# First batch of a band attention: transposing the weights unnormalized, and scaling x afterwards

## The chip, the core and the metric

The kernel runs on one core of one Trainium2 chip. The time is device microseconds of a whole execution; each kernel is timed in several runs and the median is given. The profile comes from one further execution, whose span (first to last instruction) is a little shorter than its time.

## The reference

Three stages follow one another, all in float32:

```python
# attention: 2 batches, 8 heads, 768 positions, head size 64
keep = is_global | is_local              # first 8 keys, and the last 96 keys before the query
scores = where(keep, q @ k.T / 8 + bias(head, distance), -1e9)
a = exp(scores - max(scores)); a = a / (sum(a) + 1e-9)
x = (a @ v) as 1536 tokens x 512
# feed-forward layer
h = x @ w_in                             # 512 -> 2048
x = (h * sigmoid(h)) @ w_out             # 2048 -> 512
# mixture of experts: 8 experts, each token to its best one
out[mask_e] = gate * (relu(x[mask_e] @ w1[e]) @ w2[e])
```

## The kernel before, in words

A tile is 128 queries; tiles 0 to 5 are the first batch, 6 to 11 the second. Because of the band a tile needs the keys of itself and of the tile before it (tile 0 only its own, so its score matrices are 128x128 and not 128x256). A unit is one pair of heads of one tile: unit u is head pair u%4 of tile u//4. The first batch has 24 units.

The order of the work is written out by hand. `slot_b(s)` issues the work of slot s, which belongs to several units at once: the score matmuls of unit s+1 (`emit_qk`), the bias and row maximum of unit s on VectorE (`emit_tb`, L178), the exponentials of unit s-1 on ScalarE (`emit_exp`, L188, which also sums each row into `ss`), the transposition of the weights of unit s-3 on TensorE (`emit_tr`, L212), the copy of the transposed weights out of PSUM (`emit_cp`, on ScalarE in slots 8 to 22, else on VectorE), and V's products of unit s-4 (`emit_px`, L227). V is the stationary operand there, so the result comes out transposed: features on the partitions, tokens along the free axis. In every slot from 8 to 22 VectorE also runs one operation of the decoding of the feed-forward weights (`dec_op`, L292 to L294), and in slots 0 to 6 TensorE runs two filler matmuls (`warm`, L82). Every instruction goes into the queue of its engine in this order, and each engine works its queue strictly in order.

Three pieces of this order belong to the normalization. `emit_mx` (L181) turns the row maximum into the bias of the exponential. `emit_dg` (L203 to L206) adds the small constant to the row sums of one unit, inverts them on VectorE, and lets GpSimd build for each head a diagonal matrix `dg` with these inverses. `emit_tr` then multiplies the weights with this diagonal matrix, which transposes and normalizes them in one float32 matmul. A float32 matmul appears in the trace as two instructions (so 8 for a unit with 4 blocks), a transposition through the identity, as in `gate1` (L392), as one.

When the last head pair of a tile is through (`hp==3`), `emit_xx` takes the product `pvt[n]` from PSUM through `put_xt`: ScalarE copies the high part into `xT` (L265), and VectorE subtracts it for the low part (L266). `emit_px` also calls `glob_v`, a GpSimd copy (L160) of V's rows for the global keys; `glob_k` (L157) does the same for the keys in each slot.

PSUM banks for scores, transposed weights and the like are handed out by `abank` in rotation, five of them during the slots; an instruction that takes a bank waits until the reader of its former content is done. Slots 0 to 23 run before the feed-forward layer; slots 24 to 27 are issued during its first two steps, beside its matmuls (L337 for the first layer, L357 to L359 for the second), which need `xT` and a PSUM bank named "s1" that tile 4's `pvt` also takes. During the 16 steps of the feed-forward layer's first chunk (tokens of tiles 0 to 3) VectorE decodes the rest of the weights. Later chunks and the experts follow.

Of the kernel before, what the change touches and what calls it, by code (L numbers as in the profile page):

```python
# [10 lines left out]
F32 = mybir.dt.float32  # L11
# [5 lines left out]
AF = mybir.ActivationFunctionType  # L17
ALU = mybir.AluOpType
AX = mybir.AxisListType
P = 128  # L20
# [3 lines left out]
def kernel(ctx, tc, qk, v, n_global, n_local, w_in, w_out, wg, w1, w2, out):  # L24
    nc=tc.nc
    B,NT=v.shape[0],v.shape[1]
    H=8; D=64; KC=4; FB=16; NTT=B*NT; LAG=2; LASTF=2; HB=6; PAIR=256; PX=4
# [3 lines left out]
    SB=24  # L31
    LT=3
# [10 lines left out]
    attn=es_a.enter_context(tc.tile_pool(name="attn",bufs=1,side="right"))  # L43
# [12 lines left out]
    ident=const.tile([P,P],F32,name="ident")  # L56
# [4 lines left out]
    def own_first(n): return n%3==1  # L61
# [10 lines left out]
    V=nc.vector; A=nc.scalar; G=nc.gpsimd; T=nc.tensor; S=nc.sync  # L72
# [6 lines left out]
    def warm(k):  # L79

        if not wm: wm.append(ps.tile([P,512],F32,tag="s1b",name="wm",bufs=1))
        for _ in range(k): T.matmul(wm[0].rearrange("p (a b) -> p a b",a=4),ones,ones[:,None,:].to_broadcast([P,4,P]),start=True,stop=True)  # L82
# [48 lines left out]
    def abank(shape,name):  # L131
        tg=atags[0][acnt[0]%len(atags[0])]; acnt[0]+=1
        return ps.tile(shape,F32,tag=tg,name=name,bufs=1)
# [24 lines left out]
    def glob_v(n):  # L158
        if n%NT in (0,NT-1): return
        if 4*n<SB: G.tensor_copy(vpr4[0:32,n%3,0:512],vpr4[0:32,(n-1)%3,0:512])  # L160
        else: V.tensor_copy(vpr[0:32,n%3],vpr[0:32,(n-1)%3])
    qp={}
    def emit_qk(n,hp,j):
        i=n%NT
        if (n,hp,j) in qp: return
        q=qp[n,hp,j]=abank([P,2,P],"qkp")
        sl=slice(0,2) if i else slice(0,1)
        w=ring[hp//2][j*D:(j+1)*D,hp%2]; z=ksl(n)
        T.matmul(q[:,sl],w[:,z,1],w[:,z:z+1,0] if i==0 else w[:,0:3:2,0] if z==0 else w[:,z-1:z+1,0],start=True,stop=True)  # L169
    def emit_tb(n,hp,j):  # L170
        i=n%NT; h=2*hp+j; q=qp.pop((n,hp,j))
        if j==0: tt[n,hp]=attn.tile([P,2,2,P],F32,tag="t",name="t",bufs=3) if 4*n>=SB else mp.tile([P,2,2,P],F32,tag="g",name="t",bufs=6)
        t=tt[n,hp]
        if h==0:
            mx[n]=attn.tile([P,H],F32,tag="mx",name="mx",bufs=2); ss[n]=attn.tile([P,H],F32,tag="ss",name="ss",bufs=2)
        sl=slice(0,2) if i else slice(0,1)
        tb=tabs[:,3:4,h,:] if i==0 else (tabs[:,1::-1,h,:] if i==1 else tabs[:,1:3,h,:]) if own_first(n) else tabs[:,0:2,h,:] if i==1 else tabs[:,2:0:-1,h,:]
        V.tensor_tensor_reduce(out=t[:,j,sl],in0=q[:,sl],in1=tb,scale=1.0,scalar=-3e38,op0=ALU.add,op1=ALU.max,accum_out=mx[n][:,h:h+1])  # L178
    def emit_mx(n,hp):
        h=2*hp+1  # L180
        V.tensor_scalar(out=mx[n][:,h-1:h+1],in0=mx[n][:,h-1:h+1],scalar1=-0.125,scalar2=float(np.log(1024.0)),op0=ALU.mult,op1=ALU.add)  # L181
    def emit_exp(n,hp):
        i=n%NT
        t=tt[n,hp]
        ce=1 if i==0 else 2
        for j in range(2):
            h=2*hp+j
            A.activation(out=t[:,j,:ce],in_=t[:,j,:ce],func=AF.Exp,scale=0.125,bias=mx[n][:,h:h+1],accum_out=ss[n][:,h:h+1])  # L188
    def emit_h(n,hp):
        t=tt[n,hp]; nch=ce=1 if n%NT==0 else 2  # L190
        x=attn.tile([P,2,2,nch,P],F16,tag="hl",name="hl",bufs=2); hl[n,hp]=x
        V.tensor_copy(x[:,:,0],t[:,:,:ce])
    def emit_l(n,hp):
# [2 lines left out]
        y=attn.tile([P,2,2,nch,P],F16,tag="pT",name="pT",bufs=3)  # L196
        pT[n,hp]=y
        S.dma_start_transpose(out=y.rearrange("p a b c d -> p (a b c) d"),in_=x.rearrange("p a b c d -> p (a b c d)"))
    dg={}
    def emit_dg(n,hp):  # L200

        s=ss[n][:,2*hp:2*hp+2]
        V.tensor_scalar(out=s,in0=s,scalar1=1024.0e-9,scalar2=None,op0=ALU.add)  # L203
        V.reciprocal(out=s,in_=s)
        d=attn.tile([P,2,P],F32,tag="t",name="dg",bufs=3); dg[n,hp]=d
        for j in range(2): G.tensor_scalar(out=d[:,j],in0=ident,scalar1=s[:,j:j+1],scalar2=None,op0=ALU.mult)  # L206
    def emit_tr(n,hp):

        t=tt.pop((n,hp)); d=dg.pop((n,hp)); ce=1 if n%NT==0 else 2
        m=abank([P,2,ce,P],"tp")  # L210
        for j in range(2):
            for c in range(ce): T.matmul(m[:,j,c],t[:,j,c],d[:,j],start=True,stop=True)  # L212
        y=attn.tile([P,2,ce,P],F32,tag="pT",name="pT4",bufs=3); pT[n,hp]=y
        return y,m
    def emit_cp(y,m,e):
        if e is V: V.tensor_copy(y,m)
        else: A.activation(out=y,in_=m,func=AF.Copy)
    def emit_px(n,hp):

        i=n%NT; ce=1 if i==0 else 2  # L220
        if hp==0: pvt[n]=ps.tile([P,KC,P],F32,tag="pv" if n%2 else "s1",name="px",bufs=1)
        y=pT.pop((n,hp))
        vb=[n%3] if ce==1 else [n%3,(n-1)%3] if own_first(n) else [(n-1)%3,n%3]
        for c in range(ce):
            for j in range(2):
                h=2*hp+j
                T.matmul(pvt[n][j*D:(j+1)*D,hp,:],vpr4[:,vb[c],h*D:(h+1)*D],y[:,j,c,:],start=(c==0),stop=(c==ce-1))  # L227
        if hp==3: glob_v(n)
    xlow=[]
    def emit_xx(n):  # L230
        put_xt(n,pvt[n],xlow if 4*(n+2)<SB else None)
    def emit_pv(n,hp):
        i=n%NT; ce=1 if i==0 else 2
        if hp==0: pvt[n]=ps.tile([P,H,D],F32,tag="pv",name="pv",bufs=1)
        y=pT.pop((n,hp))
        vb=[n%3] if ce==1 else [n%3,(n-1)%3] if own_first(n) else [(n-1)%3,n%3]
        for j in range(2):
            h=2*hp+j
            for c in range(ce):
                seq=[(0,0),(0,1),(0,2),(1,0),(1,1)]  # L240
                for k,(a,m) in enumerate(seq):
                    T.matmul(pvt[n][:,h,:],y[:,j,a,c,:],vpr[:,vb[c],m,h*D:(h+1)*D],start=(c==0 and k==0),stop=(c==ce-1 and k==4))  # L242
    rs={}
    def emit_rs(n,k):
        if k==0:
            rs[n]=attn.tile([P,H,1],F32,tag="rs",name="rs",bufs=2)
            V.tensor_scalar(out=rs[n][:,:,0],in0=ss[n],scalar1=1024.0e-9,scalar2=None,op0=ALU.add)
        else: V.reciprocal(out=rs[n],in_=rs[n])
    def emit_fin(n):
        r=rs.pop(n)  # L250
# [4 lines left out]
    def emit_xt(n):  # L255
# [2 lines left out]
        for k in range(KC):  # L258
            T.transpose(m[:,k,:],xa[:,2*k:2*k+2,:].rearrange("p a d -> p (a d)"),ident)
        put_xt(n,m)  # L260
    def put_xt(n,m,later=None):
        c,u=divmod(n,2)
        if u==0: xT[c]=mp.tile([P,2,KC,256],F32R,tag="xT",name="xT",bufs=3)
        sl=xT[c][:,:,:,u*P:(u+1)*P]
        A.activation(out=sl[:,0],in_=m,func=AF.Copy)  # L265
        def low(): V.tensor_tensor(out=sl[:,1],in0=m,in1=sl[:,0],op=ALU.subtract)  # L266
        if later is None: low()
        else: later.append(low)


    wraw={}; wol={}
# [357 lines left out]
    h1={}; hh={}; yp={}  # L629
# [248 lines left out]
    def want(s):  # L878
        while nl_[0]<=min(s,NS-1):
            load(nl_[0]); nl_[0]+=1  # L880
# [4 lines left out]
    npv=[SB]; fin=[]  # L885
    TB={s:[(0,2*s-2),(0,2*s-1)] for s in range(1,5)}
    for s,hs in ((5,range(3)),(6,range(3,6)),(7,range(6,8))): TB[s]=[(2,h) for h in hs]
    def slot_b(s):

        ev=[]  # L890
        n,hp=divmod(s,4); n1,h1=divmod(s-1,4); n3,h3=divmod(s-LT,4); n4,h4=divmod(s-LT-1,4)
        cur=s<SB; o1=0<=s-1<SB; o3=0<=s-LT<SB; o4=0<=s-LT-1<SB
        def a_():
            if s<SB-3: want(min(s+WL,SB-1))
            elif cur: want(s+3)
            if s==0:
                for j in range(2): emit_qk(n,hp,j)
            if cur: emit_tb(n,hp,0)
            if s+1<SB:
                for j in range(2): emit_qk(*divmod(s+1,4),j)  # L900
            if s<7: warm(2)
            if o3: cp[0]=emit_tr(n3,h3)
            if o1: emit_exp(n1,h1)
        ev.append(a_)
        def a2():
            if cur: emit_tb(n,hp,1); emit_mx(n,hp)
            if o3: emit_cp(*cp[0],A if DQ<=s<23 else V)
            if o1: emit_dg(n1,h1)
            if o4: emit_px(n4,h4)
            if xlow: xlow.pop()()  # L910
        ev.append(a2)
        def b_():
            if cur: glob_k(n,hp)
            if h4==3 and o4: emit_xx(n4)
            if s==0: table(slice(0,3))
            for d,h in TB.get(s,()): tab_heads(slice(0,2) if d==0 else slice(2,3),slice(0,2) if d==0 else slice(2,3),(h,))
            if hp==3 and 4*(n+1)<SB and cur: load_v(n+1)
        ev.append(b_)
        return ev
    cp=[None]  # L920
# [38 lines left out]
    with tc.manual_schedule():  # L959
# [11 lines left out]
        s=0  # L971
# [17 lines left out]
        for g in range(len(steps)+LAG):  # L989
            live=g<len(steps)  # L990
            if live:
                c,f=steps[g]
# [79 lines left out]
```

## Time and profile before

| | |
|---|---|
| time, median of 3 runs | 609.31 us (608.39 to 609.93) |
| profiled execution: its time, its span | 609.15 us, 607.4 us |
| busy over the span: TensorE (PE) | 590.5 us, 97% |
| weight loads of TensorE (PEld) | 498.5 us, 82% |
| VectorE (DVE) | 388.2 us, 64% |
| ScalarE (ACT) | 302.1 us, 50% |
| GpSimd (POOL) | 185.7 us, 31% |
| mean granted TensorE clock | 0.998 of full speed |

Times in the rows are microseconds from the span's start unless they are marked ns. A matmul's end is modelled, so the distance from one start to the next tells more than a duration. A mean in a group can hold instructions that waited inside the engine. Busy shares over the whole span are averages over stages that have different limits; the stage of the slots ends before 60 us.

### The profile page before, as it was taken

To read this page: it belongs to the slowest core of one execution; us is meant where nothing else is said; L and a number is where in the kernel's file an instruction comes from. 1 tells how busy PE (TensorE), PEld (TensorE's weight loads), DVE (VectorE), ACT (ScalarE), POOL (GpSimd) and SP (SyncE) were. 2 spreads that over 40 slices of the span, in tenths; PEclk is the share of its full clock that TensorE was granted. 3 is DMA by queue.
4 is the path that set the end of the run, shared out by engine and by line. 5 is a ranking of instruction groups with operands and counts; after the bars stand their busy time and mean duration, and the time that the engine had idled before them with its cause. 6 is when DMAs were issued, how large, how long until landed. Compare 5 with 4: busy or idle time off the path is not lost.

```text
span 607.4 us, 12066 instructions
## 1 busy us (share of the span) xinstructions
PE 590.5 (97%) x4078; PEld 498.5 (82%) x4078; DVE 388.2 (64%) x1074; ACT 302.1 (50%) x800; POOL 185.7 (31%) x232
## 2 busy tenths in 40 slices
PE   8998999999999999999999999999999999999995
PEld 4666888888888888888889999887888988888784
DVE  6888599998465655554543346646653877867940
ACT  7677334443444444343432325725653756776741
POOL 4678244444124341222120001212231432332321
PEclk9999999999999999999999999999999999999999
DMA  6554826788646666464434239309755558558500
GB/s 208 194 173 157 265 87 212 224 266 283 206 110 170 154 164 178 116 159 107 134 108 122 87 96 339 141 37 306 218 176 168 184 198 295 173 211 296 165 18 20
DMA packets 81226, 105.18 MB, mean 173 GB/s; under 512 B 29693, under 2 KB 44029, under 8 KB 81156
## 3 DMA queue, kind: packets, MB, share of 16 engines
q1 hardware_dynamic: 78292, 97.41, 52.0%
q0 software_dynamic: 2288, 6.39, 2.9%
q8 instruction: 34, 0.56, 0.4%
q10 hardware_dynamic: 576, 0.52, 0.3%
q14 instruction: 36, 0.29, 0.2%
HBM read 87.14 MB, written 17.99 MB: 173 GB/s over the span
## 4 chain that ended last, share of the span: by engine, by line
PE 68%; DVE 10%; issue 9%; ACT 5%; DMA 4%; POOL 3%; SPq 0%; POOLq 0%; DVEq 0%; ACTq 0%
PE s L337 17%; PE s L357 6%; PE s L358 5%; PE s L359 5%; PE h L640 4%; PE h L634 4%; PE qkp L169 4%; PE y L657 3%; PE y L659 3%; PE y L658 3%; PE tp L212 3%; POOL wol L321 2%; PE pv L242 2%; PE h L635 2%; DVE wt L294 2%
## 5 line engine op out<-in xcount | busy, mean ns | idle before, releaser
L337 PEld LDWEIGHTS s<-xT,wi 128*128 128x128 f32 x1152 | 147.3, 190 | 13.1 <-DVE g L346 6.0
L337 PE MATMUL s<-xT,wi 128*128 128x256 f32 x1152 | 152.2, 284 | 1.9 <-DVE xT L266 1.4
L342 DVE SCALAR_TENSOR_TENSOR s<-u,s 128x256 f32<-128x256 f32 x96 | 39.7, 426 | 81.4 <-ACT u L341 81.4
L341 ACT ACTIVATE u<-s 128x256 f32<-128x256 f32 x96 | 35.2, 381 | 113.6 <-PE s L337 112.7
L509 DVE TENSOR_TENSOR uq<-qr,uq 128x512 fp32r<-128x512 f32 x87 | 76.2, 898 | 7.1 <-ACT uq L508 4.3
L357 PE MATMUL s<-woh,g 128*128 128x512 f32 x192 | 79.2, 413 | 0.0
L358 PE MATMUL s<-woh,g 128*128 128x512 f32 x192 | 75.5, 393 | 0.0
L508 ACT ACTIVATE uq<-qr 128x512 fp32r<-128x512 f32 x112 | 66.4, 626 | 7.8 <-DMA qr<-in_w_dram 7.7
L346 DVE TENSOR_TENSOR g<-s,g 128x256 fp32r<-128x256 f32 x96 | 39.3, 422 | 31.6 <-ACT g L345 26.3
L657 PE MATMUL y<-uq,hh 128*128 128x512 f32 (+6 forms) x136 | 55.2, 406 | 0.0
L345 ACT ACTIVATE g<-s 128x256 fp32r<-128x256 f32 x96 | 35.6, 379 | 39.3 <-DVE s L342 39.3
L659 PE MATMUL y<-uq,hh 128*128 128x512 f32 (+6 forms) x136 | 53.7, 395 | 0.0
L658 PE MATMUL y<-uq,hh 128*128 128x512 f32 (+6 forms) x136 | 53.4, 393 | 0.0
L509 POOL TENSOR_TENSOR uq<-qr,uq 128x512 fp32r<-128x512 f32 x25 | 32.7, 1317 | 56.8 <-ACT uq L508 54.0
L188 ACT ACTIVATE t<-t,mx 128x256 f32<-128x256 f32 (+1 forms) x96 | 45.7, 480 | 0.4 <-DVE mx L181 0.4
L650 DVE SCALAR_TENSOR_TENSOR hh<-h,hh 128x224 fp32r<-128x224 f32 (+6 forms) x64 | 25.3, 395 | 31.8 <-ACT hh L649 31.8
L649 ACT ACTIVATE hh<-h 128x224 fp32r<-128x224 f32 (+6 forms) x64 | 23.2, 363 | 44.1 <-DVE h L647 23.8
L595 POOL DMA_INDIRECT out_dram<-y,ixt x17 | 17.6, 1036 | 80.3 <-ACT y L664 51.3
L357 PEld LDWEIGHTS s<-woh,g 128*128 128x128 f32 x192 | 36.3, 189 | 7.1 <-ACT u L341 2.0
L358 PEld LDWEIGHTS s<-woh,g 128*128 128x128 f32 x192 | 36.3, 189 | 5.0
L359 PE MATMUL s<-wolr,g 128*128 128x512 f32 x128 | 39.6, 391 | 0.0
L195 POOL TENSOR_TENSOR hl<-t,hl 128x512 f16<-128x512 f32 (+1 forms) x18 | 19.9, 1105 | 52.5 <-ACT gsm L435 16.4
(223 smaller groups left out, 1079.5 us busy)
## 6 DMA issues: line engine op xcount, KB each, us to landing
qr<-in_w_dram SPq DMA_DIRECT2D x128, 256.0 KB, 4.5
wolr<-wlo_d SPq DMA_DIRECT2D x64, 256.0 KB, 3.0
wiraw<-in_w_in_dram SPq DMA_DIRECT2D x16, 512.0 KB, 4.1
wraw<-in_w_out_dram SPq DMA_DIRECT2D x13, 512.0 KB, 4.5
ring<-in_qk_dram SPq DMA_DIRECT2D x22, 256.0 KB, 4.2
xe<-xe SPq DMA_DIRECT2D x7, 792.0 KB, 7.1
wlo_d<-wol SPq DMA_DIRECT2D x16, 256.0 KB, 2.9
xw<-xe SPq DMA_DIRECT2D x15, 264.0 KB, 4.7
```

The lines of the kernel that those rows point to most:

```text
L188: A.activation(out=t[:,j,:ce],in_=t[:,j,:ce],func=AF.Exp,scale=0.125,bias=mx[n][:,h:h+1],accum_out=ss[n][:,h:h+1])
L337: T.matmul(t,w[:,ww,kc,:],x[:,xx,kc,:],start=(k==0),stop=(k==11)); k+=1
L342: V.scalar_tensor_tensor(out=t,in0=u,scalar=1.0,in1=t,op0=ALU.add,op1=ALU.mult)
L346: V.tensor_tensor(out=g[:,1],in0=t,in1=g[:,0],op=ALU.subtract)
L357: T.matmul(o,g[u][:,0,sl],wh,start=(f==0),stop=False)
L358: T.matmul(o,g[u][:,1,sl],wh,start=False,stop=False)
L359: else: T.matmul(o,g[u][:,0,sl],wl,start=False,stop=(f==FB-1))
L508: A.activation(out=t[:,0],in_=r,func=AF.Copy)
L509: (G if (i%2 if pool is None else pool) else V).tensor_tensor(out=t[:,1],in0=r,in1=t[:,0],op=ALU.subtract)
L657: T.matmul(o,g[:,0,sl],w[:,0],start=(f==0),stop=False)
L658: T.matmul(o,g[:,1,sl],w[:,0],start=False,stop=False)
L659: T.matmul(o,g[:,0,sl],w[:,1],start=False,stop=(f==7))
```

## The change

For the first batch the row minimum of -0.125 times (score + bias) replaces the row maximum, so that it is the bias of the exponential as it stands; `emit_mx` is no longer called there. `emit_dg` and the diagonal matrices go. `emit_tr` transposes the raw exponentials through the identity. Once per tile, two slots after its last unit's scores, `emit_rs` inverts all eight row sums and GpSimd spreads them over 512 columns (64 per head); `emit_rb` transposes this spread tile in four pieces on TensorE and ScalarE copies it out; `emit_xx` multiplies the product `pvt` with it on VectorE, and `put_xt` is given GpSimd for both the high and the low part of `xT`. For tiles 0 to 3 `emit_rb` stands behind V's products of the tile's last unit and `emit_xx` one slot later; for tiles 4 and 5 (`own`) `emit_rb` comes one slot earlier and `emit_xx` directly behind the products, as before.

```diff
@@ emit_tb
+        if 4*n<SB: V.tensor_tensor_reduce(out=t[:,j,sl],in0=q[:,sl],in1=tb,scale=-0.125,scalar=3e38,op0=ALU.add,op1=ALU.min,accum_out=mx[n][:,h:h+1])
+        else: V.tensor_tensor_reduce(... as before ...)
@@ emit_exp
-            A.activation(..., func=AF.Exp,scale=0.125,bias=mx[n][:,h:h+1],accum_out=ss[n][:,h:h+1])
+            A.activation(..., func=AF.Exp,scale=-1.0 if 4*n<SB else 0.125,bias=mx[n][:,h:h+1],accum_out=ss[n][:,h:h+1])
-    def emit_dg(n,hp):
-        s=ss[n][:,2*hp:2*hp+2]
-        V.tensor_scalar(out=s,in0=s,scalar1=1024.0e-9,scalar2=None,op0=ALU.add)
-        V.reciprocal(out=s,in_=s)
-        d=attn.tile([P,2,P],F32,tag="t",name="dg",bufs=3); dg[n,hp]=d
-        for j in range(2): G.tensor_scalar(out=d[:,j],in0=ident,scalar1=s[:,j:j+1],scalar2=None,op0=ALU.mult)
@@ emit_tr
-            for c in range(ce): T.matmul(m[:,j,c],t[:,j,c],d[:,j],start=True,stop=True)
+            for c in range(ce): T.transpose(m[:,j,c],t[:,j,c],ident)
+    def emit_rb(n):
+        r=rs.pop(n)
+        m=abank([P,KC,P],"rb")
+        for k in range(KC): T.transpose(m[:,k,:],r[:,k*P:(k+1)*P],ident)
+        x=rb[n]=attn.tile([P,KC,P],F32,tag="t",name="xn",bufs=3)
+        A.activation(out=x,in_=m,func=AF.Copy)
     def emit_xx(n):
-        put_xt(n,pvt[n],xlow if 4*(n+2)<SB else None)
+        x=rb.pop(n)
+        V.tensor_tensor(out=x,in0=pvt[n],in1=x,op=ALU.mult)
+        put_xt(n,x,G)
@@ put_xt
+        if e: e.tensor_copy(sl[:,0],m)
+        else: A.activation(out=sl[:,0],in_=m,func=AF.Copy)
+        (e or V).tensor_tensor(out=sl[:,1],in0=m,in1=sl[:,0],op=ALU.subtract)
@@ slot_b, a2
-            if cur: emit_tb(n,hp,1); emit_mx(n,hp)
+            if cur: emit_tb(n,hp,1)
             if o3: emit_cp(*cp[0],A if DQ<=s<23 else V)
-            if o1: emit_dg(n1,h1)
+            if o3 and h3==3 and own(n3): emit_rb(n3)
             if o4: emit_px(n4,h4)
-            if xlow: xlow.pop()()
+            if o4 and h4==3 and not own(n4): emit_rb(n4)
+            if o5 and h5==3 and not own(n5): emit_xx(n5)
+            if o2 and h2==3:
+                for k in range(2): emit_rs(n2,k)
+                r=attn.tile([P,512],F32,tag="t",name="rx",bufs=3)
+                G.tensor_copy(r.rearrange("p (h d) -> p h d",h=H),rs[n2].to_broadcast([P,H,D])); rs[n2]=r
@@ slot_b, b_
-            if h4==3 and o4: emit_xx(n4)
+            if h4==3 and o4 and own(n4): emit_xx(n4)
```

## Rows read from the trace of the kernel before

**Rows 1.** Busy time of each engine by stretch, with granted clock and DMA
```profile
40.00:50.00 10.00, 9.70 (x84) 6.99 (x84) 9.26 (x36) 7.63 (x24) 7.47 (x15) 1.00 0.48 160
...
80.00:90.00 10.00, 9.93 (x59) 8.26 (x59) 9.31 (x18) 4.83 (x12) 4.10 (x4) 1.00 0.35 97
...
160.00:170.00 10.00, 10.00 (x64) 8.56 (x64) 2.92 (x12) 5.78 (x16) 0.00 (x0) 1.00 0.72 238
```

**Rows 2.** Chain that ended last, by time: start, length, engine, tile, line
```profile
11.10 0.45 PE tp L212 x4
...
21.29 1.13 PE tp L212 x8
...
36.12 1.09 PE tp L212 x8
37.20 0.59 PE px L227 x8
37.79 0.63 PE qkp L169 x4
38.42 1.10 PE tp L212 x8
...
58.03 0.61 PE px L227 x8
```

**Rows 3.** Timeline of TensorE behind the slots: start, length, line, tiles
```profile
164.73 0.66 PE L392 MATMUL gt<-ident,xr 128*128 128x128 f32 x4
165.14 0.48 PE L357 MATMUL s<-woh,g 128*128 128x512 f32 x1
```

**Rows 4.** Timeline of VectorE over slot 22
```profile
54.66 0.40 DVE L178 CUSTOM_DVE_ANT_1 t<-qkp,tabs 128x256 f32<-128x256 f32 x1
...
56.05 0.17 DVE L181 TENSOR_SCALAR mx<-mx 128x2 f32<-128x2 f32 x1
...
56.41 0.40 DVE L178 CUSTOM_DVE_ANT_1 t<-qkp,tabs 128x256 f32<-128x256 f32 x1
```

**Rows 5.** Timeline of ScalarE over parts of slots 12 and 22
```profile
30.05 0.60 ACT L265 ACTIVATE xT<-px 128x512 fp32r<-128x512 f32 x1
30.55 0.62 ACT L314 ACTIVATE wi<-wt 128x512 fp32r<-128x512 f32 x1
31.07 0.50 ACT L188 ACTIVATE t<-t,mx 128x256 f32<-128x256 f32 x1
...
54.08 0.60 ACT L217 ACTIVATE pT<-tp 128x512 f32<-128x512 f32 x1 [0.35 <-PE tp L212]
...
55.46 0.19 ACT L188 ACTIVATION_READ_ACCUMULATOR t<-t,mx 128x1 f32 x1
```

**Rows 6.** Instruction groups, 0 to 170 us: busy, mean ns, idle before
```profile
L206 POOL TENSOR_SCALAR dg<-ident,ss 128x128 f32<-128x128 f32 x48 | 28.4, 603 | 21.2 <-DVE ss L204 10.8 <-DVE mx L178 5.5 <-ACT g L345 2.3
...
L315 POOL TENSOR_TENSOR wi<-wt,wi 128x512 fp32r<-128x512 f32 x16 | 20.7, 1294 | 28.8 <-ACT wi L314 28.7
...
L160 POOL COPY vpr<-vpr 32x512 f32<-32x512 f32 x4 | 2.4, 600 | 0.0
```

**Rows 7.** Timelines of VectorE and TensorE, slot 23 to feed-forward step 1
```profile
59.29 0.69 DVE L266 TENSOR_TENSOR xT<-px,xT 128x512 fp32r<-128x512 f32 x1
...
64.98 0.74 DVE L346 TENSOR_TENSOR g<-s,g 128x256 fp32r<-128x256 f32 x2
...
72.40 0.69 DVE L266 TENSOR_TENSOR xT<-px,xT 128x512 fp32r<-128x512 f32 x1 [0.73 <-ACT xT L265]
73.01 0.69 DVE L292 TENSOR_SCALAR dct<-wiraw 128x512 int32<-128x512 int32 x1
...
60.04 3.13 PE L337 MATMUL s<-xT,wi 128*128 128x256 f32 x24 [1.42 <-DVE xT L266]
63.01 1.06 PE L212 MATMUL tp<-dg,t 128*128 128x128 f32 x8
...
66.26 3.13 PE L337 MATMUL s<-xT,wi 128*128 128x256 f32 x24
```

More of the change, by code (lines that the diff above doesn't have):

```diff
@@ L177, in emit_tb @@
         tb=tabs[:,3:4,h,:] if i==0 else (tabs[:,1::-1,h,:] if i==1 else tabs[:,1:3,h,:]) if own_first(n) else tabs[:,0:2,h,:] if i==1 else tabs[:,2:0:-1,h,:]
-        V.tensor_tensor_reduce(out=t[:,j,sl],in0=q[:,sl],in1=tb,scale=1.0,scalar=-3e38,op0=ALU.add,op1=ALU.max,accum_out=mx[n][:,h:h+1])
+        if 4*n<SB: V.tensor_tensor_reduce(out=t[:,j,sl],in0=q[:,sl],in1=tb,scale=-0.125,scalar=3e38,op0=ALU.add,op1=ALU.min,accum_out=mx[n][:,h:h+1])
+        else: V.tensor_tensor_reduce(out=t[:,j,sl],in0=q[:,sl],in1=tb,scale=1.0,scalar=-3e38,op0=ALU.add,op1=ALU.max,accum_out=mx[n][:,h:h+1])
     def emit_mx(n,hp):
@@ L187, in emit_exp @@
             h=2*hp+j
-            A.activation(out=t[:,j,:ce],in_=t[:,j,:ce],func=AF.Exp,scale=0.125,bias=mx[n][:,h:h+1],accum_out=ss[n][:,h:h+1])
+            A.activation(out=t[:,j,:ce],in_=t[:,j,:ce],func=AF.Exp,scale=-1.0 if 4*n<SB else 0.125,bias=mx[n][:,h:h+1],accum_out=ss[n][:,h:h+1])
     def emit_h(n,hp):
@@ L198, in emit_l @@
         S.dma_start_transpose(out=y.rearrange("p a b c d -> p (a b c) d"),in_=x.rearrange("p a b c d -> p (a b c d)"))
-    dg={}
-    def emit_dg(n,hp):
-        s=ss[n][:,2*hp:2*hp+2]
-        V.tensor_scalar(out=s,in0=s,scalar1=1024.0e-9,scalar2=None,op0=ALU.add)
-        V.reciprocal(out=s,in_=s)
-        d=attn.tile([P,2,P],F32,tag="t",name="dg",bufs=3); dg[n,hp]=d
-        for j in range(2): G.tensor_scalar(out=d[:,j],in0=ident,scalar1=s[:,j:j+1],scalar2=None,op0=ALU.mult)
     def emit_tr(n,hp):
-        t=tt.pop((n,hp)); d=dg.pop((n,hp)); ce=1 if n%NT==0 else 2
+        t=tt.pop((n,hp)); ce=1 if n%NT==0 else 2
         m=abank([P,2,ce,P],"tp")
         for j in range(2):
-            for c in range(ce): T.matmul(m[:,j,c],t[:,j,c],d[:,j],start=True,stop=True)
+            for c in range(ce): T.transpose(m[:,j,c],t[:,j,c],ident)
         y=attn.tile([P,2,ce,P],F32,tag="pT",name="pT4",bufs=3); pT[n,hp]=y
@@ L228, in emit_px @@
         if hp==3: glob_v(n)
-    xlow=[]
+    rb={}
+    def emit_rb(n):
[4 more added lines that the diff above has]
+        A.activation(out=x,in_=m,func=AF.Copy)
     def emit_xx(n):
-        put_xt(n,pvt[n],xlow if 4*(n+2)<SB else None)
+        x=rb.pop(n)
+        V.tensor_tensor(out=x,in0=pvt[n],in1=x,op=ALU.mult)
+        put_xt(n,x,G)
     def emit_pv(n,hp):
@@ L246, in emit_rs @@
             rs[n]=attn.tile([P,H,1],F32,tag="rs",name="rs",bufs=2)
-            V.tensor_scalar(out=rs[n][:,:,0],in0=ss[n],scalar1=1024.0e-9,scalar2=None,op0=ALU.add)
+            V.tensor_scalar(out=rs[n][:,:,0],in0=ss[n],scalar1=1e-9 if 4*n<SB else 1024.0e-9,scalar2=None,op0=ALU.add)
         else: V.reciprocal(out=rs[n],in_=rs[n])
@@ L260, in emit_xt, with put_xt @@
         put_xt(n,m)
-    def put_xt(n,m,later=None):
+    def put_xt(n,m,e=None):
         c,u=divmod(n,2)
@@ L264, in put_xt @@
         sl=xT[c][:,:,:,u*P:(u+1)*P]
[L265 to L268, printed above, removed]
+        if e: e.tensor_copy(sl[:,0],m)
+        else: A.activation(out=sl[:,0],in_=m,func=AF.Copy)
+        (e or V).tensor_tensor(out=sl[:,1],in0=m,in1=sl[:,0],op=ALU.subtract)
     wraw={}; wol={}
@@ L887, with own @@
     for s,hs in ((5,range(3)),(6,range(3,6)),(7,range(6,8))): TB[s]=[(2,h) for h in hs]
+    def own(n): return 4*(n+2)>=SB
     def slot_b(s):
         ev=[]
+        n5,h5=divmod(s-LT-2,4); o5=0<=s-LT-2<SB
         n,hp=divmod(s,4); n1,h1=divmod(s-1,4); n3,h3=divmod(s-LT,4); n4,h4=divmod(s-LT-1,4)
-        cur=s<SB; o1=0<=s-1<SB; o3=0<=s-LT<SB; o4=0<=s-LT-1<SB
+        n2,h2=divmod(s-2,4); cur=s<SB; o1=0<=s-1<SB; o2=0<=s-2<SB; o3=0<=s-LT<SB; o4=0<=s-LT-1<SB
         def a_():
```

## The prediction

> **What bounds the kernel now.** I read the busy times by stretch first, then the chain that ended last, then the timelines of each engine over one slot. In the stretches the reader is to see three stages: during the slots (the row of 40 to 50 us) TensorE and VectorE are both nearly full, ScalarE and GpSimd three quarters; at 80 to 90 us, in the feed-forward layer's first chunk, TensorE and VectorE are both full, the latter with decoding; at 160 to 170 us TensorE alone is [rows 1]. Two full engines don't tell which one sets the pace; the chain does. In the middle of the slots it never leaves TensorE: transposition, V's products, scores, next transposition, with no gap, 38.42 - 36.12 = 2.30 us from slot to slot, of which 1.09 are the transposition, 0.59 V's products and 0.63 the scores [rows 2]. From the transposition of slot 8 (21.29) to the end of V's products of slot 23 (58.03 + 0.61 = 58.64) the 16 slots take 37.35 us, 2.33 each, so stalls are small there; slots 3 to 7 take 21.29 - 11.10 = 10.19 us [rows 2]. So the change works on the stage where the bound is, and on its longest term. What follows, the decoding and the later chunks, it leaves as it is; it can only start earlier.
>
> **Transposition (TensorE).** A full unit has 8 instructions through the diagonal, 1.09 us from the first to the next operation [rows 2]. Through the identity it has 4. The trace has such a group of four: 164.73 to 165.14, 0.41 us to the next start, and that next matmul is 0.48 long, stretched by the change of kind [rows 3]. I take 0.45, so 0.64 less per full unit; the 4 units of tile 0 have half the blocks and 0.45 now [rows 2], some 0.22 less each. New is one group of four per tile for the spread sums, 0.45, or 0.11 per slot. TensorE's slot becomes 0.63 + 0.45 + 0.59 + 0.11 = 1.78 us.
>
> **VectorE.** A slot from one first `emit_tb` to the next took 1.75 us (54.66 to 56.41), of which 0.36 (56.05 to 56.41) are the bias, the constant and the inversion, all of which go; 1.39 stay [rows 4]. The low part of xT also goes, 0.69 per tile [rows 7]. New per tile are the product with the spread sums, which I set at the same 0.69 (same 512 columns, one operand in PSUM too), and one pair of constant and inversion, at most the 0.36. That is 1.39 + 1.05/4 = 1.65 a slot against 1.75 + 0.69/4 = 1.92. Row minimum with another scale instead of row maximum is the same instruction, so I cost it at nothing; if it were slower, it has 0.2 of room before VectorE sets the pace.
>
> **ScalarE.** Copy and both exponentials take 54.08 to 55.65, 1.57 us. The copy of the spread sums replaces that of the high part, 0.50 per tile, 0.13 a slot; five weight splits of 0.52 fall in the 16 slots, 0.16 a slot [rows 5]. Sum 1.86, the same before and after. That was 0.47 under TensorE; now it is the highest of the engines, and this is what is late next.
>
> **GpSimd.** 48 diagonal matrices of 603 ns go, 28.4 us. New per tile are the spread copy, the high part's copy and the low part's subtraction. The subtraction is like L315, 1.29; the copies lie between the 0.60 of L160 (512 columns, a plain copy) and four times the 603 ns of a diagonal's 128 columns, 2.4 [rows 6]. I take 0.6 to 0.7, as the row nearest to it is a copy. Then 2.6 us a tile, 0.65 a slot, replace 1.2 a slot. For tiles 0 to 3 the sums are inverted two slots before they are transposed, some 4 us, which hides even a copy of 2.4. For tile 4 there is one slot, with tile 3's two xT operations and a weight split ahead in GpSimd's queue; there TensorE, with the transposes and V's products of slots 22 and 23 behind the wait, can lose 0 to 1.3 us, and I take 0.2 within the coupling below.
>
> **The new wait.** ScalarE's copy of the spread sums stands behind V's products and four transposes: 0.59 + 0.45 - 0.49 (the copy in front of it, from the rows above) = 0.55 us if ScalarE is right behind TensorE, with the next exponentials queued behind it and the products of later units behind those. It comes once in 4 slots, 0.14 a slot; if ScalarE is late by that much anyway, it costs nothing. The shift by one bank in `abank` lets the transposes of the next slot wait for the second `emit_tb` and not for the first; VectorE, now the least loaded of the three, should be ahead of it, and I take nothing, at most one decode and one `emit_tb`, about 1 us a tile or 0.25 a slot.
>
> **Sum.** Slots 8 to 23: 1.86 + 0.14 = 2.00 a slot against 2.33, 16 x 0.33 = 5.3 us. Bounds: 1.86, no coupling, 7.5; 2.2 with both waits in full, 2.1. Slots 3 to 7: 4 x 0.22 from tile 0's units, 0.64 for the first full one, up to 0.36 of VectorE's chain where slot 7 waits for it, less 0.45 for the first spread sums: 1.4, between 0.8 and 1.7. Junction to the feed-forward layer: its first matmul waited 1.42 us for ScalarE's copy and then VectorE's subtraction from tile 4's bank [rows 7]; one VectorE operation remains, 0.7 less. Step 0 has two transpositions in front of the matmuls of step 1 (63.01 to 66.26); they lose 1.28, but the first bank is only free when L346's first half is done, 64.98 + 0.37 = 65.35, so 0.9 [rows 7]. In step 1 the decoding begins at 73.01, behind tile 5's subtraction at 72.40, which had waited 0.73 for ScalarE [rows 7]; the product can take that place, 0.6. Together 2.2, bounds 1.2 and 2.3. Total 8.9 us, from 4.1 to 11.5. Made on the profiled execution: 609.15 - 8.9 = 600.3; the median is 0.16 higher, so 600.4, with 605.2 and 597.8 as the ends. VectorE's decoding from 73 us on fills it (9.31 of 10) [rows 1] whenever it starts, so I expect the gain to reach the end whole.
>
> **Rivals.**
> First: the waits bind. The slots hang on a chain across the engines (bank shift, spread copy, GpSimd at tile 4) at 2.2 a slot, and the small terms come at their lower ends: 605.2. For it speaks that three engines are within 0.21 of each other; against it, that transposition, copy and product are whole slots apart, which leaves each engine a lead.
> Second: the coupling is nothing and ScalarE runs through at 1.86: 597.8. The wait of 0.35 that it has before a copy in slot 22 [rows 5] shows it already following TensorE, so it would have to fall behind first.
> [...]
> [...]
> Fourth: the gain is given back, because weights for the decoding arrive no earlier. Then about 609. Against it: DMA is at 0.48 of its time during the slots [rows 1], and VectorE starts decoding at 73.01 straight behind its own subtraction, not behind a transfer [rows 7].
>
> **How the numbers follow.** Forecast 0.60, first rival 0.18, second 0.10, clock 0.08, given back 0.04. The time is the forecast's, 600.4. The range takes in the first and second rival, 597.5 to 605.6, and leaves out 0.12. Within 0.3% (1.8 us, about what this kernel's measurement can tell from no change) lies only the fourth: faster 0.88, same 0.04, slower 0.08.
>
> **What would show it.** In the profile after: L212 with 88 instructions instead of 176, four in 0.4 to 0.45 us; slots of 2.0 us in the middle, with ScalarE in the chain where TensorE alone was; V's products of slot 23 ended by 52; the first feed-forward matmul about 0.7 behind them; decoding begun at about 64 and the same length from there. Wrong would be: a granted clock under 1.00 between 15 and 55 us, slots over 2.2 with TensorE waiting for `mx` or for GpSimd, or a decoding that waits for DMA.

## The result, and the profile after

The changed kernel takes 598.5 us (median of 4 runs, 597.71 to 599.75) beside 608.99 us for the kernel before on the same chip; the ratio is 0.9828, interval 0.9806 to 0.985. The forecast was 600.4, the range 597.5 to 605.6. The profiled execution of after took 599.75 us with a span of 598.0, that of before 609.15. TensorE is busy for 98% of the span, VectorE for 63%, ScalarE for 50%, GpSimd for 29%.

The busy times by stretch of the kernel after answer to [rows 1]; the columns are the same. A second slot stretch, 30 to 40 us, is added.

```profile
30.00:40.00 10.00, 10.00 (x89) 6.46 (x88) 8.68 (x31) 9.68 (x30) 7.83 (x16) 1.00 0.73 239
40.00:50.00 10.00, 9.53 (x85) 6.10 (x84) 7.89 (x30) 8.92 (x29) 5.85 (x9) 1.00 0.51 170
...
80.00:90.00 10.00, 9.95 (x66) 8.90 (x66) 9.26 (x17) 3.71 (x10) 5.04 (x4) 1.00 0.68 221
```

TensorE has no idle time between 30 and 40 us; VectorE fell from 9.26 to 7.89 between 40 and 50, ScalarE rose from 7.63 to 8.92, being asked for the same work in fewer microseconds. The granted clock stays at 1.00. At 80 to 90 us the stage behind is as it was.

TensorE's timeline of the kernel after, from the first transposition to the feed-forward layer: start, length, line, tiles, and in brackets the idle time ahead of it and what ended that. It answers to [rows 2] and to TensorE's part of [rows 7].

```profile
11.40 0.38 PE L205 MATMUL tp<-ident,t 128*128 128x128 f32 x2
...
20.44 0.63 PE L205 MATMUL tp<-ident,t 128*128 128x128 f32 x4 [0.34 <-DVE mx L178]
...
28.22 0.66 PE L205 MATMUL tp<-ident,t 128*128 128x128 f32 x4
28.81 0.66 PE L220 MATMUL px<-pT,vpr 128*64 128x128 f32 x8
29.40 0.70 PE L169 MATMUL qkp<-ring 64*128 64x256 f32 x4
30.03 0.66 PE L205 MATMUL tp<-ident,t 128*128 128x128 f32 x4
...
47.46 0.66 PE L205 MATMUL tp<-ident,t 128*128 128x128 f32 x4
48.59 0.66 PE L227 MATMUL rb<-ident,rx 128*128 128x128 f32 x4 [0.47 <-DVE mx L178]
...
50.35 0.66 PE L220 MATMUL px<-pT,vpr 128*64 128x128 f32 x8
51.87 3.14 PE L338 MATMUL s<-xT,wi 128*128 128x256 f32 x24 [0.86 <-DVE xn L232]
...
57.19 3.13 PE L338 MATMUL s<-xT,wi 128*128 128x256 f32 x24
```

A slot is 30.03 - 28.22 = 1.81 us where it was 2.30. Read by starts, since a modelled end lies behind the next start (28.22 + 0.66 = 28.88 against 28.81): the transposition takes 28.81 - 28.22 = 0.59, V's products 0.59, the scores 0.63. No bracket stands on any of them, so TensorE has no idle time between them.

VectorE's timeline of the kernel after at the end of step 1 answers to the row at 73.01 in [rows 7]: decoding begins at 63.47, straight behind the product that took the subtraction's place.

```profile
62.87 0.68 DVE L232 TENSOR_TENSOR xn<-px,xn 128x512 f32<-128x512 f32 x1
63.47 0.69 DVE L293 TENSOR_SCALAR dct<-wiraw 128x512 int32<-128x512 int32 x1
```

The same points of both traces, subtracted, give where the time came from (before, after, won, forecast; us). The transposition of slot 3 begins at 10.94 in TensorE's timeline of before; the chain of [rows 2] enters it at 11.10.

| Section | before | after | won | forecast |
|---|---|---|---|---|
| entry to the transposition of slot 3 | 10.94 | 11.40 | -0.46 | 0 |
| slots 3 to 7 | 21.29 - 10.94 = 10.35 | 20.44 - 11.40 = 9.04 | 1.31 | 1.4 |
| slots 8 to 23, to the wait ahead of the first feed-forward matmul | 60.04 - 1.42 - 21.29 = 37.33 | 51.87 - 0.86 - 20.44 = 30.57 | 6.76 | 5.3 |
| that wait | 1.42 | 0.86 | 0.56 | 0.7 |
| step 0 | 66.26 - 60.04 = 6.22 | 57.19 - 51.87 = 5.32 | 0.90 | 0.9 |
| step 1 to the first decode | 73.01 - 66.26 = 6.75 | 63.47 - 57.19 = 6.28 | 0.47 | 0.6 |
| rest of the profiled execution | 609.15 - 73.01 = 536.14 | 599.75 - 63.47 = 536.28 | -0.14 | 0 |
| sum | 609.15 | 599.75 | 9.40 | 8.9 |

The profiled execution of after is the slowest of its four, so this pair shows 9.40 us where the medians lie 10.5 apart.

### The profile page after: what moved, and what is told of

It reads as the page before. It is cut to its first block, busy times and chain, and to the rows that moved or that the text cites. A ratio compares the mean times of both kernels' runs of the same rounds, so it can differ in the third digit from the quotient of the medians.

```text
span 598.0 us, 11816 instructions
## 1 busy us (share of the span) xinstructions
PE 583.9 (98%) x4014; PEld 490.0 (82%) x4014; DVE 378.9 (63%) x1014; ACT 300.8 (50%) x800; POOL 172.1 (29%) x202
## 5 line engine op out<-in xcount | busy, mean ns | idle before, releaser
L510 DVE TENSOR_TENSOR uq<-qr,uq 128x512 fp32r<-128x512 f32 x87 | 71.1, 840 | 7.5 <-ACT uq L509 4.7
```

What stands on the lines that cost most here:

```text
L510: (G if (i%2 if pool is None else pool) else V).tensor_tensor(out=t[:,1],in0=r,in1=t[:,0],op=ALU.subtract)
```

## The experiments

The theory: the slots are faster because TensorE's slot is shorter. The rival that grew out of the runs: much of it is the small work taken from VectorE, which the forecast had put off the path. All edits are to the kernel after unless it says otherwise; medians are given with the ratio to the kernel before in the same job, which took 608.86 to 609.27.

**The old work put back on scratch tiles** (bias, constant and inversion on VectorE, two diagonals on GpSimd per unit; nothing reads them):

```diff
+ def emit_dg(n,hp):   # s and d: tiles of their own
+     V.tensor_scalar(out=s,in0=ss[n][:,2*hp:2*hp+2],scalar1=1024.0e-9,scalar2=None,op0=ALU.add)
+     V.reciprocal(out=s,in_=s)
+     for j in range(2): G.tensor_scalar(out=d[:,j],in0=ident,scalar1=s[:,j:j+1],scalar2=None,op0=ALU.mult)
  if cur:
      emit_tb(n,hp,1)
+     V.tensor_scalar(out=y,in0=mx[n][:,2*hp:2*hp+2],scalar1=-0.125,scalar2=float(np.log(1024.0)),op0=ALU.mult,op1=ALU.add)
...
+ if o1: emit_dg(n1,h1)
```

> The changed kernel with the removed side work put back on scratch tiles: per unit the bias operation, the constant and the inversion on VectorE and the two diagonal matrices on GpSimd, none of them read by anything. The transposes stay single. Theory (the slots run at TensorE's pace, so what VectorE and GpSimd were spared is not the gain): VectorE's slot grows from about 1.65 to 2.0 us against TensorE's 1.81 plus a quarter of 0.59, so 598.5 to 600.5 us. Rival (the relief of VectorE and GpSimd is the gain): 605 us or more, most of the way back to 609.

Measured: 612.15, ratio 1.0049 (1.0032 to 1.0066), slower than the kernel before, which neither theory had. Its timeline, all engines:

```profile
30.79 0.60 POOL L160 COPY vpr<-vpr 32x512 f32<-32x512 f32 x1
...
30.80 2.01 DVE L918 TENSOR_SCALAR my<-mx 128x2 f32<-128x2 f32 x1
...
31.34 0.20 POOL L157 COPY ring<-ring 128x32 f32<-128x32 f32 x1
31.52 1.26 POOL L322 TENSOR_TENSOR wi<-wt,wi 128x512 fp32r<-128x512 f32 x1
...
34.06 0.66 PE L205 MATMUL tp<-ident,t 128*128 128x128 f32 x4 [1.32 <-DVE mx L178]
```

An operation on 2 columns, 0.17 us elsewhere, takes 2.01: it ends at 32.81, when GpSimd's three operations in a row end (31.52 + 1.26 = 32.78). The next `emit_tb` is queued behind it, and TensorE's transposes wait 1.32 for that. But GpSimd carried the old and the new work at once here (9.67 of 10 us at 40 to 50), which neither kernel does, so the run shows that such a wait occurs and not its share; the next ones separate the parts.

**The transposition as a two-pass matmul** again, all else kept:

```diff
- T.transpose(m[:,j,c],t[:,j,c],ident)
+ T.matmul(m[:,j,c],t[:,j,c],ident,start=True,stop=True)
```

> The changed kernel with each transposition as an ordinary float32 matmul with the identity, so two instructions again; nothing goes back on VectorE or GpSimd. Theory (TensorE's pace): 1.09 for 0.59 us per full unit, half of that for tile 0, 20 x 0.50 + 4 x 0.25 = 11 us more, 608.5 to 610. Rival (relief of the other engines): 599 to 602.

Measured: 608.36, ratio 0.9997 (0.9984 to 1.0009). TensorE's timeline:

```profile
33.33 1.16 PE L205 MATMUL tp<-ident,t 128*128 128x128 f32 x8
...
35.64 1.16 PE L205 MATMUL tp<-ident,t 128*128 128x128 f32 x8
```

The slot is 2.31 again. Without the single-pass transposes nothing is won.

**Each transposition issued twice**:

```diff
- for c in range(ce): T.transpose(...)
+ for c in [c for c in range(ce) for _ in range(2)]: T.transpose(...)
```

> The changed kernel with each transposition of the weights issued twice into the same place. Measures what one transposition costs where the slots run at TensorE's pace. 88 instructions more. If one costs 0.146 us (four in 0.585, as in the slots after): +12.8 us, 611.3. If 0.104 (four in 0.41 us, as the prediction read it behind the slots): +9.2, 607.7. If ScalarE had become the bound with TensorE 0.08 below it, as the prediction said, 1.3 us less than either.

Measured: 607.41, ratio 0.9973 (0.9961 to 0.9984), 8.9 us above the kernel after, 8.9 / 88 = 0.101 for each added transposition. TensorE's timeline, then the busy times of that stretch:

```profile
32.87 1.09 PE L205 MATMUL tp<-ident,t 128*128 128x128 f32 x8
...
35.11 1.09 PE L205 MATMUL tp<-ident,t 128*128 128x128 f32 x8
```

```profile
30.00:40.00 10.00, 10.00 (x89) 7.01 (x88) 6.62 (x23) 8.11 (x24) 6.25 (x11) 1.00 0.55 185
```

Slots of 2.24 against 1.81: four more transposes cost 0.44 at once, and they cost it although all other engines had room. So TensorE is the bound of the slot after the change. And 0.11 each, four of them 0.44, leaves 0.59 - 0.44 = 0.15 that a group pays once. About 1.03 of 2.24 us are transposes here and the clock stays at 1.00.

**The transposes of the spread sums issued twice** (`for k in (0,0,1,1,2,2,3,3)`):

> The changed kernel with the four transposes of the spread sums issued twice. Theory (TensorE's pace, no slack): 24 instructions more at 0.146 us, of which those of tile 5 stand beside the feed-forward matmuls: +2.9 to 3.5 us, 601.4 to 602. Rival of the prediction (ScalarE is the bound at 1.86 to 2.00 a slot and TensorE has room): under +1 us.

Measured: 602.63, ratio 0.9893 (0.9877 to 0.991). TensorE's timeline:

```profile
25.18 0.66 PE L205 MATMUL tp<-ident,t 128*128 128x128 f32 x4
...
26.36 1.09 PE L227 MATMUL rb<-ident,rx 128*128 128x128 f32 x8
...
28.02 0.66 PE L205 MATMUL tp<-ident,t 128*128 128x128 f32 x4
```

That slot is 2.84 against 28.22 - 25.83 = 2.39 after, 0.45 more. Four such slots are 1.8 us, and the group of tile 5, in step 1, is 0.4. Decoding begins at 65.00, 1.53 later than after, although the transposition of slot 3 came 0.63 earlier (10.77), so 2.16 are lost between these two points: the rival's "under +1 us" is out. The medians lie 4.1 apart; what adds the rest stays open.

**Only the transposes, on the kernel before** (diagonals still built; the exponentials' bias holds a constant per head pair):

```diff
- T.matmul(m[:,j,c],t[:,j,c],d[:,j],start=True,stop=True)
+ T.transpose(m[:,j,c],t[:,j,c],ident)
```

> The kernel before with one edit: the weights of the first batch go through the identity and not through the diagonal matrix, which is still built and read by nothing. Left out of the computation: the normalization of the first batch; each head pair is divided by a constant near its mean row sum (in the exponential's bias) so that the experts get about the same numbers of tokens. Side work on VectorE and GpSimd is that of before. Theory (TensorE was the bound, and the others follow close behind): slots at the highest of TensorE 1.81, VectorE 1.92, GpSimd 1.95 a slot, so 600 to 602 us. Rival (small operations of VectorE and the diagonals of GpSimd hold each other up, so that their removal is needed for the gain): slots stay over 2.15, 604 to 609.

Measured: 607.26, ratio 0.9977 (0.9962 to 0.9992). The timeline of all engines, and the busy times (the clock is the last but two):

```profile
25.79 0.66 PE L212 MATMUL tp<-ident,t 128*128 128x128 f32 x4
...
27.60 0.66 PE L212 MATMUL tp<-ident,t 128*128 128x128 f32 x4
...
28.44 2.03 DVE L181 TENSOR_SCALAR mx<-mx 128x2 f32<-128x2 f32 x1
...
29.18 1.26 POOL L315 TENSOR_TENSOR wi<-wt,wi 128x512 fp32r<-128x512 f32 x1
...
31.72 1.12 PE L212 MATMUL tp<-ident,t 128*128 128x128 f32 x4 [1.32 <-DVE mx L178]
```

```profile
30.00:31.00 1.00, 0.40 (x4) 0.00 (x0) 0.96 (x4) 0.44 (x2) 0.51 (x2) 1.00 0.70 201
31.00:32.00 1.00, 0.28 (x2) 0.28 (x3) 1.00 (x4) 0.66 (x4) 1.00 (x2) 0.74 1.07 430
32.00:33.00 1.00, 1.00 (x6) 0.67 (x7) 0.93 (x6) 0.07 (x1) 0.27 (x2) 0.50 1.04 284
33.00:38.00 5.00, 5.00 (x28) 2.93 (x26) 3.39 (x15) 3.33 (x10) 3.29 (x7) 0.50 0.59 187
```

Where nothing waits the slots are 1.81, as after. Then the bias stands 2.03 us beside GpSimd, which ends its split at 30.44; TensorE is idle; and its clock falls to 0.50, till 38. The clock has a part in the time: two slots take 38.23 - 31.72 = 6.51 at 0.50, and 3.62 at 1.00. But the execution with the highest mean clock of the ten, 0.996, took 606.63, so the waits bind beside it; how much each costs is not separated. So the short transposition is needed but wins little by itself: the kernel before has VectorE waits that its 2.31 us slot mostly covered (its L181 has a mean of 276 ns and L203 of 227 over the slots) and a 1.81 us slot doesn't.

**Only VectorE's three small operations put back**: the first edit without the diagonals on GpSimd.

> The changed kernel with only VectorE's three small operations per unit put back on scratch tiles (bias, constant, inversion, read by nothing); GpSimd as in the changed kernel. By count alone VectorE's slot becomes 2.0 us against TensorE's 1.81 plus a quarter of 0.59: 599 to 600.5. Rival, from the run with all side work back, where such an operation took 2.0 us beside GpSimd's copies: these operations wait until GpSimd's running instruction ends, 0.3 to 0.6 us a slot more, 603 to 608.

Measured: 608.59, ratio 0.9995 (0.9984 to 1.0006): just above the rival's 603 to 608 and far from 599 to 600.5. These three operations, some 0.36 us a slot, cost all that the change won. Three of the ten executions kept a mean clock of 0.999, and took 607.47 to 608.73, so the loss is there without a fall of the clock. The next two runs take its two kinds of wait apart.

**The inversion one slot later**, so that it doesn't wait for sums of exponentials of its own slot (an edit to the last run, with the three operations back):

```diff
- if o1: emit_sx(n1,h1)
+ if o2: emit_sx(n2,h2)
```

> The run with VectorE's three small operations put back (608.59 us), but with constant and inversion taken one slot later, so that they no longer wait for the exponentials that ScalarE runs in the same slot. They still go from SBUF to SBUF beside GpSimd. Theory A (the gain hung on freeing VectorE from ScalarE's sums of the same slot): back to 599 to 601.5. Theory B (it hung on small SBUF operations that wait until GpSimd's instruction ends): 605 or more.

Measured: 604.91, ratio 0.993 (0.9907 to 0.9954).

**The three operations as reciprocals**, of the same 128x2, at the same places (again an edit to the run with the three operations back):

```diff
- V.tensor_scalar(out=s,in0=ss[n][:,2*hp:2*hp+2],scalar1=1024.0e-9,scalar2=None,op0=ALU.add)
+ V.reciprocal(out=s,in_=ss[n][:,2*hp:2*hp+2])
...
- V.tensor_scalar(out=y,in0=mx[n][:,2*hp:2*hp+2],scalar1=-0.125,scalar2=float(np.log(1024.0)),op0=ALU.mult,op1=ALU.add)
+ V.reciprocal(out=y,in_=mx[n][:,2*hp:2*hp+2])
```

> The same run with all three small operations as inversions, a form that shows no long waits beside GpSimd in the traces (166 ns in the mean, where the bias operation has 366); the inversion of the sums still waits for the exponentials of the same slot. Theory A: stays at 605 or more. Theory B: back to 599 to 601.5. If both are needed, both runs stay over 603.

Measured: 605.34, ratio 0.9929 (0.9905 to 0.9953). The groups of instructions up to 60 us in these three runs (busy time, mean ns of one, idle time before and its releaser), first with the three operations back, then one slot later, then as reciprocals:

```profile
L916 DVE TENSOR_SCALAR my<-mx 128x2 f32<-128x2 f32 x24 | 7.4, 309 | 0.8
...
L224 DVE TENSOR_SCALAR sx<-ss 128x2 f32<-128x2 f32 x22 | 3.7, 170 | 2.9 <-ACT t L189 2.9
```

```profile
L916 DVE TENSOR_SCALAR my<-mx 128x2 f32<-128x2 f32 x24 | 6.9, 287 | 0.8
...
L224 DVE TENSOR_SCALAR sx<-ss 128x2 f32<-128x2 f32 x22 | 4.2, 191 | 0.0
```

```profile
L916 DVE RECIPROCAL my<-mx 128x2 f32<-128x2 f32 x24 | 4.0, 166 | 0.8
...
L224 DVE RECIPROCAL sx<-ss 128x2 f32<-128x2 f32 x23 | 3.5, 153 | 3.7 <-ACT t L189 3.6
```

One slot later the wait for ScalarE is gone and the stretched bias stays; as reciprocals the bias is never stretched and the wait for ScalarE stays. Each run keeps one of the two waits and gains only 3.7 and 3.3 of the 10.1 us; with either alone 6.4 and 6.8 remain, so neither wait by itself is the gain. A run without both waits, with the three operations kept, was not made, so what their plain count costs is not shown. The wait of the weights' transposes for `mx` is 6.7 us with the three back, 4.0 and 3.9 in the others, 0.3 after. With the two together the profiled execution also lost the clock: TensorE waits 1.60 before a transposition at 55.46, and in the busy times of that run it is then granted 0.59 and 0.50:

```profile
55.00:60.00 5.00, 4.20 (x24) 2.97 (x26) 2.88 (x15) 2.69 (x7) 1.74 (x2) 0.59 0.36 108
60.00:66.00 6.00, 5.21 (x29) 4.81 (x26) 1.77 (x5) 0.38 (x1) 4.13 (x20) 0.50 0.72 206
```

In the other two no stretch from 10 to 66 us is below 1.00.

**The spread sums transposed ahead of V's products for all tiles, and x's product one slot earlier** (`def own(n): return True`):

> The changed kernel with all tiles treated like tiles 4 and 5: spread sums transposed one slot earlier, straight behind the weights' transposes, and the product directly behind V's products. Theory (TensorE's pace; eight transposes in a row cost 0.45 us more and not 0.59, as the doubled transposes showed): 4 x 0.14 us less, 598.0. Rival (the spread sums, now due one slot after the inversion, are not ready because GpSimd is at the tile before): TensorE waits 0.3 to 0.5 us a tile, 599.5 to 600.5.

Measured: 600.91, ratio 0.9863 (0.9842 to 0.9884). TensorE's timeline:

```profile
24.00 0.60 PE L227 MATMUL rb<-ident,rx 128*128 128x128 f32 x4
...
25.75 0.66 PE L205 MATMUL tp<-ident,t 128*128 128x128 f32 x4
...
28.20 0.66 PE L205 MATMUL tp<-ident,t 128*128 128x128 f32 x4 [0.57 <-DVE mx L178]
```

The turns of tiles 1 to 3 each cost TensorE a wait of 0.57 that the kernel after does not have. It is for VectorE's `mx`, where the rival had the spread sums. That tiles 0 to 3 come one slot later is worth about 2.4 us by the medians.

**The other bank for the first feed-forward matmul**:

```diff
- i=pst.get('n',0); pst['n']=i+1
+ i=pst.get('n',1); pst['n']=i+1
```

> The changed kernel in which the first feed-forward matmuls take the bank s1b and the second ones the bank s1, which tile 4's product still holds; nothing else changes. Theory (the first feed-forward matmul waits only for that bank, 0.86 us in the profile after): all of the 0.86 us goes, 597.7. Rival (it would wait for something else right behind, or TensorE's order gives it back at step 1): under 0.3 us.

Measured: 598.27, ratio 0.9825 (0.9807 to 0.9843). TensorE's timeline:

```profile
49.73 0.66 PE L220 MATMUL px<-pT,vpr 128*64 128x128 f32 x8
50.31 3.13 PE L338 MATMUL s<-xT,wi 128*128 128x256 f32 x24
```

The wait at the junction is gone, 0.94 won from the last transposition to here, and decoding begins at 61.90 (0.63 of its lead is an earlier entry). In the medians this can't be told from the kernel after.

**Fillers for four slots and not seven** (`if s<4: warm(2)`):

> The changed kernel with filler matmuls in slots 0 to 3 only, not in 4 to 6. Theory (TensorE's pace also in slots 4 to 6, with ScalarE at about 1.6 against 1.76 us): 3 x 0.1 to 0.2, 598.0 to 598.3. Rival (the clock, with a quarter to a third of the work in transposes, needs the fillers): granted clock under 1.00 somewhere between 12 and 25 us, 600 us or more.

Measured: 598.2, ratio 0.9817 (0.9797 to 0.9837). The mean granted clock of its executions is 0.997 to 0.998, against 0.998 to 0.999 in the kernel after; in TensorE's timeline a unit's scores take 0.70 at 13.19 and at 20.80, as in the kernel after at 29.40, where the clock is 1.00. No difference that can be told.

**Both small edits together**:

> The changed kernel with both small edits that did no harm alone: the first feed-forward matmuls take the bank s1b, and no filler matmuls in slots 4 to 6. From the two profiles 0.9 us at the junction and 0.3 to 0.5 us before it: 597.0 to 597.6, a ratio to the kernel before of 0.980 to 0.982. If the medians of the single edits (598.27 and 598.2) are all there is, 598.0 and no difference from the changed kernel.

Measured: 597.75 (597.35 to 598.68), ratio 0.9824 (0.981 to 0.9838). It beats the kernel before; against the kernel after (0.9828) nothing is shown.

## Why the prediction was right in its total, and where it was not

**The bound and the stage.** Right: 6.76 of the 9.40 us lie in slots 8 to 23, and no stage behind them changed (536.14 and 536.28). But "stalls are small there" was read from a mean, 2.33, over 16 slots of which the last two have no scores and are shorter. The first 14 took (55.22 - 21.29) / 14 = 2.42, so some 1.7 us of them are stalls. The largest stands in VectorE's and TensorE's timelines of before, where the inversion waits for ScalarE and the work behind it holds up a transposition:

```profile
32.18 0.37 DVE L203 TENSOR_SCALAR ss<-ss 128x2 f32<-128x2 f32 x1 [1.10 <-ACT t L188]
...
33.74 1.16 PE L212 MATMUL tp<-dg,t 128*128 128x128 f32 x8 [0.79 <-DVE mx L178]
...
55.22 1.13 PE L212 MATMUL tp<-dg,t 128*128 128x128 f32 x8
```

Of the 33.93 - 27.02 = 6.91 us won in these 14 slots, TensorE's own work gives 14 x (1.09 - 0.59) - 3 x 0.59 = 5.2; the other 1.7 are these stalls, which the kernel after doesn't have. The prediction saw only 2.33 - 2.30 = 0.03 a slot of them.

**"I take 0.45" for a transposition.** Mis-sized. In the slots four take 0.59, by starts, against the 0.41 of the row it came from [rows 3]. An added one costs 0.10 to 0.11; 0.15 a group is paid once, beside the change of kind on both sides. The prediction saw that the next matmul in [rows 3] was stretched, and allowed only 0.04 for it.

**"ScalarE ... is the highest of the engines", 1.86 and with 0.14 of coupling 2.00 a slot.** This is the step that failed. ScalarE's timeline of the kernel after:

```profile
30.23 0.50 ACT L189 ACTIVATE t<-t,mx 128x256 f32<-128x256 f32 x1
...
31.22 0.58 ACT L210 ACTIVATE pT<-tp 128x512 f32<-128x512 f32 x1
31.70 0.50 ACT L189 ACTIVATE t<-t,mx 128x256 f32<-128x256 f32 x1
```

Copy and both exponentials come round in 31.70 - 30.23 = 1.47, not 1.57: the prediction added up to the end of the last one, while the next starts 0.10 before that. With the prediction's 0.13 and 0.16 for the other copies that is 1.76, an estimate. TensorE, at 0.63 + 0.59 + 0.59 = 1.81 plus 0.59 per tile for the spread sums (0.15 a slot), is above it. From slot 8 to slot 22 it took 47.46 - 20.44 = 27.02 us, and 14 x 1.81 + 3 x 0.59 = 27.1: it has no gap in all that time. So the coupling of 0.14 cost TensorE nothing there. ScalarE's slot, then, was forecast at 2.00 and is 1.76, TensorE's at 1.78 and is 1.96 with the spread sums; the higher one counts, and the two errors of opposite sign nearly cancel: 1.93 a slot up to slot 22, and 1.91 over all 16, the last two of which have no scores.

**VectorE and GpSimd.** The prices were right: the product took 0.68 to 0.69 (0.69 set), and on GpSimd the subtraction and the spread copy took 1.28 and 0.62 (set at 1.29, and at 0.6 to 0.7). These are in the timelines of the kernel after, with an operation of VectorE's between them:

```profile
45.46 1.28 POOL L269 TENSOR_TENSOR xT<-xn,xT 128x512 fp32r<-128x512 f32 x1
...
45.91 0.86 DVE L249 TENSOR_SCALAR rs<-ss 128x8 f32<-128x8 f32 x1
...
47.92 0.62 POOL L918 COPY rx<-rs 128x512 f32<-128x512 f32 x1
```

The worth was not. The prediction set VectorE at 1.92 before and 1.65 after, below the bound both times, and gave its relief nothing in slots 8 to 23. The runs show that the gain needs it as much as the transposition: each without the other leaves 607 to 609 us (two-pass 608.36, only transposes 607.26, three operations back 608.59). The counts missed two waits inside VectorE's in-order queue: small operations that stretch beside GpSimd (2.01 and 2.03 us where one takes 0.17), and an inversion that waits for exponentials of the same slot (1.10 at 32.18). A slot of 2.31 us hid most of them (0.79 at 33.74 is what showed), a slot of 1.81 does not. The forecast was right because the change removes both parts, not because it had seen this; so far it was luck. One such operation is left, the constant added to a tile's sums (L249): 6 of them have a mean of 577 ns. The one shown takes 0.86, until GpSimd's subtraction ends at 45.46 + 1.28 = 46.74. VectorE then works without a gap until 48.59, where TensorE's wait of 0.47 for `mx` ends, so this operation may still cost that wait; no run tried it.

**The small terms.** Slots 3 to 7, junction, step 0 and step 1 came within 0.14 of their terms in the profiled pair. Not foreseen is 0.46 lost before slot 3: the filler matmuls at 6.45 take 0.96 to the next start, against 0.53 at 5.55 before. Among the profiled executions of the changed kernel and of the variants that leave VectorE's work alone (eight) that transposition starts between 10.74 and 11.40, so it varies by itself by more than this loss.

**The rivals.** Waits that bind, 2.2 a slot: not seen; from the start of slot 8 to the junction TensorE waits only 0.34 (20.44) and 0.47 (48.59). No coupling, 597.8: nearest to the measured time, but for another reason, as ScalarE is not the bound. The clock: it stayed at 1.00 through the slots. The run with every transposition doubled (46% of the slot, at 1.00) shows that such a share cost no clock; a larger share was not tried. What went ahead of each fall seen up to 80 us was TensorE waiting, 1.32 to 2.42 us. Given back: no, the rest of the execution is equal to 0.14.

## What to carry to other kernels

When the bound of a stage gets shorter, go through each in-order queue for waits that the old slot covered, and not for counts only: an engine at 1.92 of 2.31 us may still stall a slot of 1.81 by one operation that lasts 2 us. Take an engine's slot from start to start of a back-to-back stretch, and the price of a group from the stretch in which it will stand, with the changes of kind around it. An edit that does little alone is no evidence against it: here both halves were needed.

## What the runs showed of the hardware

- A 128x2 TENSOR_SCALAR on VectorE takes 0.17 us, and took 2.01 and 2.03 beside GpSimd. These two end within 0.03 us of the last of three GpSimd operations in a row (at 30.79, 31.34 and 31.52 in the run with the old work; at 28.46, 29.01 and 29.18 in that with transposes alone). A RECIPROCAL of the same shape at the same places had a mean of 153 to 166 ns, and took at most 0.17 us in VectorE's timeline from 25 to 40 us. What makes the one wait and not the other was not tried.
- Up to 80 us TensorE's granted clock fell to 0.50 four times in the profiles of three runs, each time during a wait of TensorE or within 0.5 us after it: 1.32 us at 31.72 and 2.42 at 59.10 (transposes alone), 1.60 at 55.46 (three operations back) and 1.74 at 59.59 (old work put back). It stayed there for some 7, 3, 10 and 10 us; 24 feed-forward matmuls took 5.19 to 5.24 us in the last two and not 3.13. Yet waits of about the same length cost no clock: 1.42 before 60.04 in the kernel before [rows 7], 1.32 at 34.06 with the old work put back, 1.68 at 57.55 with the inversion one slot later, 1.47 at 57.95 with reciprocals. So the length of one wait does not tell them apart. What does was not tried, and stays open.
